# Loading the first four units' r and k without their gap rows, with three smaller moves beside it

## The chip, the cores and the metric

The kernel runs on one core of a Trainium2 chip. The metric is device time in microseconds (us) of one execution; less is better. The shown time of a kernel is the median of several executions.

## The reference, cut to what matters

Three stages follow one another. The first is a recurrence with a decaying state (4 batches, 8 heads, 768 steps, head size 48); the other two are feed-forward blocks over the 3072 tokens (384 to 2048 to 384).

```
for t in range(S):
    kt, vt, rt = (k[:, :, t], v[:, :, t], r[:, :, t])
    cur = np.einsum('bhd,bhe->bhde', u[None] * kt, vt)
    y[:, :, t] = np.einsum('bhd,bhde->bhe', rt, state + cur)
    state = w[None, :, :, None] * state + np.einsum('bhd,bhe->bhde', kt, vt)
h = x @ w_in;  g = h * np.tanh(softplus(h));  x = g @ w_out
h = np.maximum(x @ w_in, 0.0);  out = h * h @ w_out
```

## The kernel before

**Units.** The recurrence is done in chunks of 128 steps. A unit is one chunk of one batch: 6 chunks by 4 batches give 24 units; units 0 to 3 are the first chunk, and the feed-forward work can only begin when their y is there. For a unit, r and k lie transposed in a tile rk of 112 partitions by 1024 float32: even heads in rows 0 to 47, odd heads in rows 64 to 111, and rows 48 to 63, the gap rows, are zeros that come from memory with the rest. One transfer brings a tile (448 KB). The values v (192 KB) and the natural-order k (192 KB) of units 0 to 3 are further transfers; later units load a whole nat tile (576 KB).

**The work on a unit of the first chunk.** `products` (L474 VectorE, L479 TensorE, L482 VectorE) multiplies r by k over all 112 rows and sums them with u to the diagonal dg. `rk_scale` (L462, VectorE) scales the 112 rows with powers of the decay, the table E, which `tables` (L284 to L304, VectorE) makes from w. `scores` (L541, TensorE) multiplies k by r from rows 0 to 47 and 64 to 111. `fill` writes dg on the anti-diagonal of a tile A, for even heads (e = 0) and odd heads (e = 1): by ScalarE in four instructions (L514) or by VectorE in one (L520). `select` (L550, VectorE) puts the scores into A by a mask. `y_pe` (L598, L601, TensorE) makes y, and `y_out` (L685, L687, L694) splits it in two parts, xh and xl, which feed the first block.

**The feed-forward blocks.** The hidden dimension has 16 tiles of 128; a column of 512 tokens against a tile j is a step i. A step's up product is nine matrix products (`mm3`, L815 to L817: high by high, high by low, low by high, for three depths). After the gate function (ScalarE L852, L862, L871; VectorE L877) the result g is split in ghi (L909) and glo (L914), and the down product is again nine matrix products. For the steps in `FULL` it isn't: g stays float32, is not split, and the down product is three float32 products (L939), which the profile records as six. Before, `FULL` holds steps 0 to 6. Weights come as 64-bit floats (raw, 768 KB a tile) and are turned into high and low parts by ScalarE (L371, L377, L412) and VectorE (L381, L388, L410, L415).

**What sets the order.** `Plan.order` (L144) simulates the engines with a duration and a due time for each item, and the program is issued in the order that comes out. Every engine then runs its queue in that order; an instruction that waits holds up all behind it. All of the loads concerned are issued by SyncE (SP), through `dma` (L261). A semaphore wait comes from each true dependence. Units 0 to 3 load by `load_unit` (L436), with due times -180 + 10 n; raw weights of the first block follow with -140 + j; each natural k has -136.5 + n. `first` (L309) issues the table of w before all that. VectorE first zeroes `idle` (L329), on which TensorE runs 11 products (L327) while the loads come. GpSimd (POOL) zeroes four small pieces of the states (L318) and the tile pads (L655), and copies parts of v into pads (L663).

Of the kernel before, what the change touches and what calls it, by code (L numbers as in the profile page):

```python
# [20 lines left out]
B, H, S, D = 4, 8, 768, 48  # L21
# [16 lines left out]
GROUP_OF = [(sum(GROUPS[:g]), n) for g, n in enumerate(GROUPS) for _ in range(n)]  # L38
HIGH, WHIGH = 32, 2
WACT = frozenset(range(5, 9))  # L40
FULL = frozenset(range(0, 7))


class Tl:
# [165 lines left out]
def rwkv_moe_kernel(ctx: ExitStack, tc: tile.TileContext, good, rk, nat, wuT, wrow, ub, cst, w1, w2, out):  # L210
    nc = tc.nc
# [46 lines left out]
    add = plan.add  # L258

    def dma(o, i, eng=nc.sync):  # L260
        eng.dma_start(out=o, in_=i)  # L261
# [59 lines left out]
    idle = const.tile([128, 512], BF16, name="idle")  # L321
    T_idle = fixed(idle, "idle")
# [3 lines left out]
        for _ in range(n):  # L326
            nc.tensor.matmul(o, idle[:, 0:128], idle, start=True, stop=True, skip_group_check=True)  # L327

    add("DVE", 0.2, -199, lambda: nc.vector.memset(idle, 0.0), w=[T_idle])  # L329
    t = R["acc2"].new([128, 512], F32, "idle_ps")  # L330
    add("PE", 4.5, -199, lambda t=t: busy(t.get(), 11), r=[T_idle], w=[t])

# [8 lines left out]
    t = R["at"].new([128, NP, 128], F32, "tps")  # L341
# [14 lines left out]
    def convert(layer, j, due, load_due):  # L356

        raw = R[f"w{j}"].new([128, 768, 2], U32, f"raw{layer}_{j}")
        t, hi, lo = parts(layer, j)
        f = WF[layer, j] = R["wf"].new([128, 768], F32, f"wf{layer}_{j}")  # L360
        src = (w1, w2)[layer - 1][j]
# [31 lines left out]
            )  # L393

        it = add("SP", 0.786, load_due, load, w=[raw])
        if layer == 2:
            gates.append((it, int(load_due)))
        elif j >= 6:
            gates.append((it, -1))
# [28 lines left out]


    ups = {}  # L430
    units = [(c, b) for c in range(NCH) for b in range(B)]
    NU = len(units)
    U = {}
# [2 lines left out]
    def load_unit(n, due):  # L436
        u = U[n] = {}
        if n < B:
            t = u["rk"] = R[("rk", "rk", "w12", "w14")[n]].new((HP, 2, NP, C), F32, f"rk{n}")
            v = u["nat"] = R[("nat", "w11", "w13", "w15")[n]].new((128, 3, H, D), F32, f"nat{n}")  # L440
            u["k"], u["v"] = (v.part(lambda ap, i=i: ap[:, i]) for i in (1, 2))
            src = rk[n, :, 0:2 * NP * C].rearrange("q (i p t) -> q i p t", i=2, p=NP)
            add("SP", 0.69, due, lambda: dma(t.get(), src), w=[t])
            add("SP", 0.29, due, lambda: dma(u["v"].get(), nat[n][:, 2]), w=[u["v"]])
            ups[-1] = add("SP", 0.29, -136.5 + n, lambda: dma(u["k"].get(), nat[n][:, 1]), w=[u["k"]])
            return
        for x, shape, src, mb in (("rk", (HP, 2, NP, C), rk[n, :, 0:2 * NP * C].rearrange("q (i p t) -> q i p t", i=2, p=NP), 0.69), ("nat", (128, 3, H, D), nat[n], 0.88)):
            t = u[x] = R[x].new(shape, F32, f"{x}{n}")
            def load(t=t, src=src):
                dma(t.get(), src)  # L450

            it = add("SP", mb, due, load, w=[t])
            gates.append((it, int(due)))
        u["k"] = u["v"] = u["nat"]
# [50 lines left out]
    def fill(n, e, due):  # L505

        u = U[n]
        A = u["A", e] = R["glo" if n in (1, 3) else "A"].new([128, NP, C], F32, f"A{n}_{e}")

        def f():  # L510
            a = A.get()
            for p in range(NP):
                h = 2 * p + e
                nc.scalar.activation(a[:, p, :], anti, AF.Copy, scale=u["dg"][:, h:h + 1])  # L514

        if 2 <= n < B and e or units[n][0] == 1 and not e:

            def g():
                d = u["dg"].ap.rearrange("q (p e) -> q e p", e=2)[:, e, :]
                nc.vector.tensor_tensor(  # L520
                    A.get(), anti[:, None, :].to_broadcast([128, NP, C]), d[:, :, None].to_broadcast([128, NP, C]), ALU.mult
                )

            add("DVE", 0.69, due, g, r=[u["dg"], T_cst], w=[A])
            return
        add("ACT", 1.56, due, f, r=[u["dg"], T_cst], w=[A])
# [509 lines left out]
    t = R["acc2"].new([128, 512], F32, "idle_ps2")  # L1036
# [307 lines left out]
```

## Time and profile before

| what | value |
|---|---|
| median of three executions | 915.09 us (912.25 to 916.12) |
| the profiled execution, its own time | 915.5 us |
| its span in the profile | 913.7 us |
| TensorE busy | 901.0 us of it, 99% |
| VectorE busy / ScalarE busy | 549.2 us / 582.6 us |
| read from memory / written to it | 100.27 MB / 29.88 MB |

The span runs from the first instruction to the last; the profiled execution's own time has 1.8 us around it. A busy share is an average over the whole span: the first 30 us are another stage than the rest, and each stage has to be read by itself. In the profile's lists, an idle time in square brackets stands before the instruction that it delayed, with what released that instruction. SPq is the queue of SyncE, which issues transfers.

### The profile page before, as it was taken

What the parts mean: (1) busy time and instruction counts of PE and PEld (TensorE: products, weight loads), DVE (VectorE), ACT (ScalarE), POOL (GpSimd) and SP (SyncE); (2) the same over time, 40 slices, a digit from 0 to 9 for tenths busy, and PEclk for the clock granted to TensorE, in tenths of its full rate; (3) what the DMA queues carried; (4) which work ended last, traced back from release to release, by engine and by line L of the source; (5) the groups of instructions that cost most, each with busy time, mean ns of one, the idle gap of its engine ahead of it and who ended that gap; (6) DMA issues with size and microseconds to landing.
All of it is one profiled execution on the core that took longest, in us unless ns stands there. A gap on an engine that the chain in (4) does not pass through costs nothing.

```text
span 913.7 us, 13422 instructions
## 1 busy us (share of the span) xinstructions
PE 901.0 (99%) x5228; PEld 756.4 (83%) x5228; DVE 549.2 (60%) x911; ACT 582.6 (64%) x1059; POOL 3.9 (0%) x13
## 2 busy tenths in 40 slices
PE   8999999999999999999999999999999999999997
PEld 6666788789898988788888888888888888899997
DVE  8999947999343448678885323224677876211212
ACT  5999768896455567778775554544677866544442
POOL 1000000000000000000000000000000000000000
PEclk9999999999999999999999999999999999999999
DMA  9996416994226654022665110655300355200001
GB/s 288 350 374 239 155 63 221 368 393 193 69 83 221 224 186 149 1 56 75 214 219 185 47 56 17 203 199 193 104 9 1 103 185 195 70 1 1 35 0 39
DMA packets 34537, 132.09 MB, mean 145 GB/s; under 512 B 3905, under 2 KB 8258, under 8 KB 34466
## 3 DMA queue, kind: packets, MB, share of 16 engines
q1 hardware_dynamic: 34178, 130.76, 42.0%
q8 instruction: 43, 0.70, 0.3%
q10 hardware_dynamic: 288, 0.39, 0.1%
q14 instruction: 28, 0.23, 0.1%
HBM read 100.27 MB, written 29.88 MB: 142 GB/s over the span
## 4 chain that ended last, share of the span: by engine, by line
PE 91%; DMA 5%; DVE 2%; ACT 1%; issue 0%; SPq 0%; DVEq 0%
PE h L815 14%; PE h L817 14%; PE h L816 14%; PE acc L976 7%; PE acc L978 7%; PE acc L977 7%; PE acc L815 7%; PE acc L817 6%; PE acc L816 6%; DMA nat<-in_nat_dram 3%; PE sc L541 2%; PE y L611 2%; PE acc L939 1%; PE y L588 1%; DMA raw<-in_w_dram 1%; PE y L644 1%
## 5 line engine op out<-in xcount | busy, mean ns | idle before, releaser
L914 DVE TENSOR_TENSOR glo<-g,ghi 128x512 fp32r<-128x512 f32 x96 | 66.4, 692 | 216.9 <-ACT ghi L906 213.4
L922 ACT ACTIVATE e<-h 128x512 f32<-128x512 f32 x96 | 57.4, 597 | 174.5 <-PE h L817 174.5
L906 ACT ACTIVATE ghi<-e 128x512 fp32r<-128x512 f32 x96 | 59.7, 622 | 19.9 <-PE acc L977 19.9
L914 DVE TENSOR_TENSOR glo<-e,ghi 128x512 fp32r<-128x512 f32 x89 | 60.2, 691 | 17.0 <-ACT ghi L911 14.5
L923 ACT ACTIVATE g<-e 128x512 f32<-128x512 f32 x96 | 60.7, 632 | 2.9
L897 DVE TENSOR_TENSOR e<-e,r 128x512 f32<-128x512 f32 x64 | 44.2, 691 | 26.2 <-ACT r L896 25.9
L892 ACT ACTIVATE e<-h 128x512 f32<-128x512 f32 x64 | 37.9, 592 | 32.3 <-PE h L817 32.0
L514 ACT ACTIVATE A<-cst_sb,dg 128x128 f32<-128x128 f32 x168 | 52.9, 392 | 2.7 <-DVE dg L482 2.6
L911 ACT ACTIVATE ghi<-e 128x512 fp32r<-128x512 f32 x64 | 40.2, 628 | 21.7 <-DVE e L890 21.6
L895 ACT ACTIVATE r<-e 128x512 f32<-128x512 f32 x64 | 40.1, 627 | 15.9 <-DVE e L884 15.9
L887 DVE SCALAR_TENSOR_TENSOR r<-e,r 128x512 f32<-128x512 f32 x64 | 44.2, 691 | 1.7
L890 DVE SCALAR_TENSOR_TENSOR e<-r,h 128x512 f32<-128x512 f32 x64 | 43.9, 686 | 1.7
L976 PE MATMUL acc<-w,ghi 128*128 128x384 f32 x128 | 44.2, 345 | 0.0
L978 PE MATMUL acc<-w,glo 128*128 128x384 f32 x128 | 43.2, 337 | 0.0
L977 PE MATMUL acc<-w,ghi 128*128 128x384 f32 x128 | 43.1, 337 | 0.0
L893 ACT ACTIVATE e<-e 128x512 f32<-128x512 f32 x64 | 40.4, 631 | 1.7
L896 ACT ACTIVATE r<-r 128x512 f32<-128x512 f32 x64 | 40.3, 629 | 1.4
L550 DVE COPY_PREDICATED A<-cst_sb,sc 128x512 f32<-128x512 int32 x48 | 33.9, 734 | 12.1 <-PE sc L541 12.1
L815 PE MATMUL h<-xh_a,w 128*128 128x512 f32 x96 | 39.7, 413 | 0.0
L462 DVE TENSOR_TENSOR rk<-rk,E 112x1024 f32<-112x1024 f32 x24 | 29.3, 1221 | 17.2 <-DMA rk<-in_rk_dram 17.2
L815 PE MATMUL h<-xh_b,w 128*128 128x512 f32 x96 | 37.7, 393 | 0.6 <-DVE e L877 0.6
L816 PE MATMUL h<-xl_a,w 128*128 128x512 f32 x96 | 37.5, 391 | 0.2 <-DVE xl_a L694 0.2
(510 smaller groups left out, 2495.6 us busy)
## 6 DMA issues: line engine op xcount, KB each, us to landing
raw<-in_w_dram SPq DMA_DIRECT2D x32, 768.0 KB, 10.4
wd<-w SPq DMA_DIRECT2D x32, 768.0 KB, 9.0
nat<-in_nat_dram SPq DMA_DIRECT2D x20, 576.0 KB, 5.1
rk<-in_rk_dram SPq DMA_DIRECT2D x24, 448.0 KB, 5.0
out_dram<-o SPq DMA_DIRECT2D x22, 192.0 KB, 2.0
w_0r<-wd SPq DMA_DIRECT2D x4, 768.0 KB, 4.3
w_1r<-wd SPq DMA_DIRECT2D x4, 768.0 KB, 5.7
w_2r<-wd SPq DMA_DIRECT2D x4, 768.0 KB, 5.5
```

The costliest lines, as they stand in the source:

```text
L514: nc.scalar.activation(a[:, p, :], anti, AF.Copy, scale=u["dg"][:, h:h + 1])
L815: nc.tensor.matmul(o, wh, xh, start=first, stop=False, skip_group_check=True)
L816: nc.tensor.matmul(o, wh, xl, start=False, stop=False, skip_group_check=True)
L817: nc.tensor.matmul(o, wl, xh, start=False, stop=last, skip_group_check=True)
L887: nc.vector.scalar_tensor_tensor(r.ap, e.ap, 2.0, r.ap, ALU.subtract, ALU.mult)
L906: add("ACT", 0.63, due, lambda: nc.scalar.activation(hi.get(), square.ap, AF.Square), r=[square], w=[hi])
L914: lambda: nc.vector.tensor_tensor(lo.get(), g.ap, f32v(hi.ap), ALU.subtract), r=[g, hi], w=[lo],
L922: add("ACT", 0.59, d, lambda: nc.scalar.activation(e.get(), h.ap, AF.Relu), r=[h], w=[e])
L923: add("ACT", 0.63, d + 0.2, lambda: nc.scalar.activation(g.get(), e.ap, AF.Square), r=[e], w=[g])
L976: nc.tensor.matmul(o, hi[:, sl], h_, start=(j == 0), stop=False, skip_group_check=True)
L977: nc.tensor.matmul(o, hi[:, sl], l_, start=False, stop=False, skip_group_check=True)
L978: nc.tensor.matmul(o, lo[:, sl], h_, start=False, stop=(j == NF - 1), skip_group_check=True)
```

## The change

- Units 0 to 3 load rk in two transfers, rows 0 to 47 and rows 64 to 111 (192 KB each). Rows 32 to 63 are zeroed on the chip before: by VectorE for units 0 and 1, by GpSimd for units 2 and 3. The loads wait for that, since rows 32 to 47 are written by both. The zeroing of `idle` gets an earlier due time, so that it stays first on VectorE.
- The order of these loads is fixed: rk0, rk1, v0, rk2, v1, rk3, v2, v3, then the first raw weights. Before, it was rk0, v0, rk1, v1, rk2, v2, rk3, v3. The first raw weights come ahead of the natural k of all four units, the other raw weights of the first block after v3.
- `FULL` loses step 6: six steps stay unsplit.
- The fill of unit 1's odd heads goes from ScalarE to VectorE.

```diff
-FULL = frozenset(range(0, 7))
+FULL = frozenset(range(0, 6))
...
-    add("DVE", 0.2, -199, lambda: nc.vector.memset(idle, 0.0), w=[T_idle])
+    add("DVE", 0.2, -240, lambda: nc.vector.memset(idle, 0.0), w=[T_idle])
...
         it = add("SP", 0.786, load_due, load, w=[raw])
+        if layer == 1 and not j:
+            order = [first_loads[k] for k in sorted(first_loads)] + [it]
+            for p, q in zip(order, order[1:]):
+                q["after"].append(p)
+            for q in later:
+                q["after"].append(it)
+        elif layer == 1:
+            it["after"].append(first_loads[B + 0.5])
...
-            add("SP", 0.69, due, lambda: dma(t.get(), src), w=[t])
-            add("SP", 0.29, due, lambda: dma(u["v"].get(), nat[n][:, 2]), w=[u["v"]])
+
+            def load():
+                for q in (0, 64):
+                    dma(t.get()[q:q + D], src[q:q + D])
+
+            if n >= 2:
+                add("POOL", 0.95, -230 + n, lambda: nc.gpsimd.memset(t.get()[32:64], 0.0), w=[t])
+            else:
+                add("DVE", 0.4, -230 + n, lambda: nc.vector.memset(t.get()[32:64], 0.0), w=[t])
+            first_loads[n] = add("SP", 0.59, -180 + 2 * n, load, w=[t])
+            first_loads[n + 1.5] = add("SP", 0.29, -177 + 2 * n, lambda: dma(u["v"].get(), nat[n][:, 2]), w=[u["v"]])
             ups[-1] = add("SP", 0.29, -136.5 + n, lambda: dma(u["k"].get(), nat[n][:, 1]), w=[u["k"]])
+            later.append(ups[-1])
...
-        if 2 <= n < B and e or units[n][0] == 1 and not e:
+        if 1 <= n < B and e or units[n][0] == 1 and not e:
```

## Rows read from the trace of the kernel before

**Rows 1.** The page, busy time of each engine in the span.
```profile
PE 901.0 (99%) x5228; PEld 756.4 (83%) x5228; DVE 549.2 (60%) x911; ACT 582.6 (64%) x1059; POOL 3.9 (0%) x13
```

**Rows 2.** Waits of TensorE, whole span: waited for, us in total, times, longest.
```profile
PE y L598 <- DVE A L550: 2.7, 1, 2.7
PE acc L939 <- DVE g L877: 1.9, 2, 1.0
```

**Rows 3.** The chain that ended last, first 60 us: start, us, what.
```profile
29.55 14.25 DMA nat<-in_nat_dram
...
51.68 0.61 DVE g L877
...
52.33 2.84 PE acc L939 x6
```

**Rows 4.** Windows of 5 us: PE, PEld, DVE, ACT, POOL busy, PEclk, DMA share, GB/s.
```profile
5.00:10.00 5.00, 5.00 (x37) 3.95 (x35) 3.28 (x8) 0.49 (x1) 1.64 (x2) 1.00 1.05 266
...
15.00:20.00 5.00, 4.85 (x72) 4.28 (x70) 4.93 (x9) 4.00 (x11) 0.00 (x0) 1.00 1.04 402
...
25.00:30.00 5.00, 5.00 (x45) 3.98 (x42) 4.61 (x7) 3.66 (x7) 0.00 (x0) 0.74 1.05 396
```

**Rows 5.** VectorE in order of time, first 45 us: start, us, what [idle before, releaser].
```profile
0.88 0.27 DVE L329 MEMSET idle<- 128x256 uint32 x1 [0.88 <-PEq L1327]
2.37 0.17 DVE L284 TENSOR_SCALAR wu_sb<-wu_sb 112x4 f32<-112x4 f32 x1 [1.22 <-DMA wu_sb<-in_wuT_dram]
...
5.44 0.16 DVE L304 COPY w<-Ex 112x4 f32<-112x4 f32 x1
6.74 0.69 DVE L474 TENSOR_TENSOR pr<-rk 112x512 f32<-112x512 f32 x1 [1.13 <-DMA rk<-in_rk_dram]
...
9.24 0.69 DVE L474 TENSOR_TENSOR pr<-rk 112x512 f32<-112x512 f32 x1 [0.55 <-DMA rk<-in_rk_dram]
...
11.73 0.69 DVE L474 TENSOR_TENSOR pr<-rk 112x512 f32<-112x512 f32 x1 [0.54 <-DMA rk<-in_rk_dram]
...
18.01 0.69 DVE L520 TENSOR_TENSOR A<-cst_sb,dg 128x512 f32<-128x512 f32 x1
...
43.89 0.56 DVE L493 TENSOR_TENSOR nat<-nat,ub_sb 128x384 f32<-128x384 f32 x1 [1.45 <-DMA nat<-in_nat_dram]
```

**Rows 6.** SyncE's queue in order of time: start, us, transfers issued.
```profile
1.67 0.43 SPq L261 DMA_DIRECT2D rk<-in_rk_dram  x1
2.15 0.43 SPq L261 DMA_DIRECT2D nat<-in_nat_dram  x1
...
6.73 3.62 SPq L261 DMA_DIRECT2D raw<-in_w_dram  x4
```

**Rows 7.** GpSimd and ScalarE in order of time.
```profile
7.59 1.38 POOL L655 MEMSET pads<- 128x1536 f32 x1 [6.60 <-PE tps L336]
...
13.15 2.45 ACT L514 ACTIVATE A<-cst_sb,dg 128x128 f32<-128x128 f32 x8 [0.65 <-DVE dg L482]
```

**Rows 8.** TensorE in order of time: down products of steps 6 and 8.
```profile
80.16 2.73 PE L939 MATMUL acc<-g,wf 128*128 128x512 f32 x6
82.82 0.44 PE L588 MATMUL y<-rk,S 48*64 48x128 f32 x8
...
91.19 0.40 PE L815 MATMUL acc<-ghi,w 128*128 128x512 f32 x1
91.43 0.40 PE L816 MATMUL acc<-glo,w 128*128 128x512 f32 x1
...
93.36 0.38 PE L541 MATMUL sc<-rk 48*128 48x128 f32 x2
```

**Rows 9.** VectorE in order of time, splits of steps 8 and 9.
```profile
89.43 0.44 DVE L909 CAST ghi<-e 128x512 fp32r<-128x512 f32 x1
...
90.22 1.30 DVE L914 TENSOR_TENSOR glo<-e,ghi 128x512 fp32r<-128x512 f32 x2
```

**Rows 10.** One window, 45 to 113 us, columns as in rows 4.
```profile
45.00:113.00 68.00, 66.88 (x452) 47.34 (x453) 67.95 (x112) 58.25 (x94) 0.00 (x0) 1.00 0.67 252
```

More of the change, by code (lines that the diff above doesn't have):

```diff
@@ L430, in rwkv_moe_kernel @@
     ups = {}
+    first_loads, later = {}, []
     units = [(c, b) for c in range(NCH) for b in range(B)]
```

## The prediction

> **What bounds the kernel now.** I read the page's busy times first: TensorE is busy 901.0 of 913.7 us [rows 1], so only what moves its work as a whole, shortens it, or removes one of its waits can count. Its waits come next [rows 2]: 2.7 us once for the select of the first chunk, and 1.9 us in two waits for g. That is nearly all there is to win besides an earlier start.
>
> The chain of waits says what sets the first 52 us [rows 3]. It runs through transfers, the last of which is the nat tile of unit 4, issued at 29.55 and 14.25 us on its way. VectorE sits idle 1.45 us for it until 43.89 [rows 5], and the gate products (g, L877) queued behind it reach TensorE late; at 52.33 TensorE goes on [rows 3]. From there to the end it is busy nearly without a gap. So the arrival of nat4 plus VectorE's work behind it sets the end; anything earlier counts only if it moves that arrival, or eats more than VectorE's 1.45 us.
>
> The windows show why transfers matter: the DMA share is full (1.05) both from 5 to 10 us, at 266 GB/s, and from 15 to 20 us, at 402 GB/s [rows 4]. The slow stretch is that of rk and v. VectorE waits for rk0 until 6.74, for rk1 until 9.24, for rk2 until 11.73 [rows 5]: a step of 2.5 us for rk and v together, 640 KB or 0.655 MB, 262 GB/s. By bytes (448 of 640) rk's part of it is 1.75 us.
>
> **The change part by part.**
>
> *Zeroing on the chip.* A zeroing of 256 elements a row took VectorE 0.27 us [rows 5]; 1024 elements are worked out as 1.08 us. VectorE is then free of the first at 0.88 + 0.27 + 1.08 = 2.23 and of the second at 3.31. SyncE issued rk0 at 1.67 [rows 6]; now it waits there for the first zeroing, until about 2.3, and everything behind it in its queue waits too: **+0.6 us** on the start of all loads. The ends are 0 (the zeroing takes under 0.5 us) and 1.6 (both zeroings come ahead of it, 3.31 less 1.67). The engines had nothing but the small constants to move by then, so nothing hides it. rk1 would be issued at 2.3 and two more issues of 0.48 (the spacing in [rows 6]), 3.26, against 3.31: hidden by rk0's own transfer. The decay tables start at 3.31 instead of 2.37 and so end near 6.5 instead of 5.6 [rows 5]; they are needed after the first product, at 6.74 + 0.69. Hidden, with 0.9 us of cover; past that it would cost one for one. GpSimd's two take 1024/1536 of 1.38 us each [rows 7], 0.92, and end before 3; rk2 is the sixth issue, after 4.6. Hidden. TensorE's first tables wait likewise; nothing needs them early.
>
> *Twice four loads instead of four.* Four more issues of 0.48 us are 1.9 us of SyncE's time. At that spacing the eight loads are issued by 5.5; then it stood until rk0 had landed (6.74 [rows 5]) before the first raw weights, at 6.73 [rows 6]. With the two small tables before them done, eight seem to stand open at a time. Eight halves of 192 KB are 6 us of work at 262 GB/s: the engines don't run dry, so the issues cost nothing. Were they to run dry, it would be the 1.9.
>
> *Fewer bytes.* 64 KB a unit, 256 KB or 0.26 MB in all. If the rate stays 262 GB/s a pair of halves takes 384/448 of 1.75, 1.50 us: 0.25 a unit, 1.0 us in all. But the same full engines move 402 GB/s of weights, so it isn't bytes alone that fill them during rk. A load of 48 rows, all within one half of the partitions, is shown by no row. The nearest rows for the dear end: a half-range load at half of the weights' rate, 201 GB/s, makes 0.393 MB / 201 = 1.96 us a pair, +0.21 a unit, **+0.84** in all; at the extreme a half takes as long as a whole does now, +7.0. Between 1.50 and 1.96 I take the middle, 1.73, which is the 1.75 of now: **0**.
>
> The Trainium skill, page "SBUF — State Buffer", in the section "Can I just issue two DMAs to hit both halves?", speaks against this edit: one load from partition 0 on and one from 64 on were only 6% faster together than one, since each reaches half of the ports. With its 196 GB/s for 64 partitions that is an estimate of 208 GB/s, 1.89 us a pair, +0.6 instead of my 0. No row here loads one half alone, so the trace neither bears it out nor refutes it.
>
> *Values one load later.* v0 comes behind rk1, about 1.7 us later; it is read only after the fill and the selects of its unit. rk1 to rk3 come ahead of one v each (0.75 us). VectorE waited 0.55 and 0.54 us for rk1 and rk2 [rows 5]; those go, and VectorE's next wait takes them up.
>
> *One more fill on VectorE.* +0.69 us there [rows 5], ScalarE loses four of the eight in 2.45 us [rows 7], 1.2 us. VectorE is busy 4.93 of 5 us around it [rows 4], so the first chunk's select comes later and TensorE's 2.7 us wait grows; TensorE then runs partly at the lower of its two clocks, as before (granted 0.74 between 25 and 30 us [rows 4]). All this is upstream of nat4: 0.6 and 0.69 are 1.29, under the 1.45 us of idle before 43.89. **0**; without that cover 0.69.
>
> *Step 6 split.* TensorE: the float32 down product takes from 80.16 to 82.82, 2.66 us; a split one from 91.19 to 93.36, 2.17 [rows 8]: −0.49. VectorE: a cast of 0.44 and half of 1.30 [rows 9], +1.09, in a stretch in which it is busy 67.95 of 68 us [rows 10]. Step 8's glo is done at about 90.87 [rows 9] and read at 91.43 [rows 8]: 0.56 us of slack, against 1.09 + 0.49 that the two engines move apart. At worst TensorE waits 1.02, a net +0.53; at best −0.49. VectorE's weight work may be reordered around it: I take the middle, **0**.
>
> **Sum.** +0.6 for the wait of the first load, carried by the chain of transfers to nat4 and on to TensorE. The profiled execution took 915.5 us (1.8 around its span of 913.7), 0.4 over the median. 915.09 + 0.6 = **915.7 us**; its own ends, 0 to 1.6 for the wait and 0.5 either way for step 6, give 914.6 to 917.2. A measurement of this kernel can hardly tell less than 0.5%, 4.6 us, from no change.
>
> **Rivals.**
>
> *Bytes decide* (faster). The rate stays and the pair costs 1.50 us: −1.0 + 0.6, and step 6 gives its 0.49 because VectorE's order leaves the glo in time: −0.9, **914.2 us**. For it: the DMA engines are full without a gap, so less to move is less time. Against: the wait at the start takes back more than half. At the far end nat4 comes so early that both waits for g vanish, −1.9 − 0.49, 912.7.
>
> *Half a range at a time* (slower). Each half load reaches only part of the ways into the memory, and the engines queue for it: +0.84 to the chain and +0.6 at the start, **916.5 us**; the place is SyncE's first six loads, and it decides as soon as a pair takes over 1.75 us. For it: loads of rk already run 1.5 times slower than weights at the same DMA share. Against: no row shows a half load. By the skill's section named above the sum would be 916.3. Twice this price, with step 6 and the fill uncovered, is 918.6.
>
> *VectorE becomes the bound* (slower). It gets 0.69 early and 1.09 in its full stretch; if nat4 is no longer the last to arrive, both come out at TensorE: 0.6 + 0.69 + 0.53, **916.9 us**. For it: rows 10. Against: the 1.45 us of idle.
>
> **How the numbers follow.** The forecast (no net gain) 0.42, bytes 0.33, half ranges 0.17, VectorE 0.08. The range goes from the far end of the second to that of the third, 912.7 to 918.6. Beyond 0.5% on the fast side would need three times the waits for g gone, or the stretch of low clock with them: 0.04. On the slow side half loads far dearer than half the weights' rate: 0.08. Between, 0.88.
>
> **What would show it.** In the changed profile: VectorE's zeroings of 32 by 1024 near 1.08 us; rk0's first issue near 2.3 instead of 1.67; the first product (L474) at about 7.3 instead of 6.74; the third at most 1.7 us behind the second, against 2.49; the first raw weights landing within 1 us of 16.6; nat4's reader (L493) at about 44.5; TensorE's waits for g again near 2 us; six rather than seven of the float32 down products. I am wrong if the zeroings take half of that, if the products come before 6.5, or if L493 moves by over 1 us either way.

## The result, and the profile after

The changed kernel took **921.12 us** (median of 22 runs, 914.70 to 923.54) beside 916.12 (22 runs, 912.25 to 920.03) for the kernel before, run beside it. The ratio is 1.0059, with a 95% interval of 1.0045 to 1.0072: slower by 5.4 us, where 0.6 was forecast, and beyond the range. The profiled execution took 921.36 us, with a span of 919.6, against 915.5 and 913.7 before. Line numbers of the old code move by 19 from L462 on (L474 is now L493, L493 is L512, L815 is L834, L939 is L958).

The page of the changed kernel: busy times, and the granted TensorE clock in 40 slices.

```profile
PE 904.8 (98%) x5229; PEld 761.0 (83%) x5231; DVE 552.5 (60%) x916; ACT 580.7 (63%) x1055; POOL 6.6 (1%) x15
...
PEclk7899999999999999999999999999999999999999
```

TensorE is busy 3.8 us longer than in [rows 1], with one product more on record: of the 5.9 us that the span grew, 3.8 are added busy time (slower products, less what the split of step 6 saves) and 2.1 are idle time. The clock is below 9 in the first two slices; before, all 40 are 9. Windows of 5 us, first of the changed kernel (columns as in [rows 4]):

```profile
5.00:10.00 5.00, 3.15 (x25) 2.64 (x23) 3.83 (x10) 0.49 (x1) 2.04 (x2) 1.00 1.02 223
10.00:15.00 5.00, 4.67 (x37) 3.52 (x39) 4.97 (x9) 3.38 (x12) 1.72 (x4) 0.62 1.05 283
15.00:20.00 5.00, 5.00 (x32) 3.72 (x28) 3.38 (x5) 2.85 (x4) 0.54 (x1) 0.50 1.04 399
20.00:25.00 5.00, 5.00 (x36) 4.76 (x38) 3.21 (x7) 2.09 (x5) 0.00 (x0) 0.50 1.04 396
25.00:30.00 5.00, 4.50 (x52) 4.28 (x51) 3.71 (x8) 2.78 (x8) 0.00 (x0) 0.68 1.04 393
```

The same view of the kernel before, with windows that were not shown ahead of the prediction:

```profile
5.00:10.00 5.00, 5.00 (x37) 3.95 (x35) 3.28 (x8) 0.49 (x1) 1.64 (x2) 1.00 1.05 266
10.00:15.00 5.00, 4.79 (x50) 3.70 (x50) 4.46 (x8) 4.30 (x15) 1.84 (x3) 1.00 1.05 288
...
20.00:25.00 5.00, 2.27 (x29) 1.96 (x29) 5.00 (x9) 5.00 (x10) 0.00 (x0) 0.92 1.03 391
```

The clock column is the one to read, with one warning. The clock record in the trace begins only when the clock first rises, at 7.1 us before and at 4.3 after. Until then a window shows 1.00, although the products on zeros (listed below) take 0.44 us each before, about twice as long as later. From that rise on TensorE held the full 2.4 GHz until 24.2 us before. After, the clock falls at 11.2 us and stays at 0.50, the 1.2 GHz level, until 28.2. Twice (1 − PEclk) times the length of each window, added up, gives the time at the lower level behind the first rise: 3.4 us in the first 30 before, 17.0 after. With the time up to the first rise, it is about 10.5 us before and 21.4 after. Being busy did not bring the clock back here: from 15 to 25 us TensorE is busy all the time in the changed kernel and stays at 0.50. And one window ahead of the fall TensorE, which before had been busy for all of its 5 us, is busy for 3.15.

What it waited for there stands in TensorE's own order of time (start, us, what, idle before and releaser), changed kernel:

```profile
1.20 4.07 PE L327 MATMUL idle_ps<-idle 128*128 128x512 bf16 x11 [1.20 <-DVE idle L329]
6.30 1.15 PE L336 MATMUL tps<-cst_sb,Ex 112*128 112x112 f32 x8 [1.02 <-DVE Ex L293]
...
9.32 1.02 PE L498 MATMUL dgp<-wu_sb,pr 112*128 112x2 f32 x8 [0.77 <-DVE pr L493]
...
35.81 0.50 PE L835 MATMUL h<-xl_a,w 128*128 128x512 f32 x1 [1.16 <-DVE xl_a L713]
...
57.16 5.42 PE L958 MATMUL acc<-g,wf 128*128 128x512 f32 x12
...
72.72 0.50 PE L834 MATMUL h<-xh_a,w 128*128 128x512 f32 x1 [1.79 <-DVE g L896]
...
74.89 2.74 PE L958 MATMUL acc<-g,wf 128*128 128x512 f32 x6
```

The same view of the kernel before:

```profile
1.20 4.88 PE L327 MATMUL idle_ps<-idle 128*128 128x512 bf16 x11 [1.20 <-DVE idle L329]
5.87 1.65 PE L336 MATMUL tps<-cst_sb,Ex 112*128 112x112 f32 x8
...
30.80 0.50 PE L816 MATMUL h<-xl_a,w 128*128 128x512 f32 x1 [0.22 <-DVE xl_a L694]
...
69.61 2.74 PE L939 MATMUL acc<-g,wf 128*128 128x512 f32 x6
```

Before, the eleven products on zeros (L327) ran until 6.08 us, past the moment at which VectorE had finished what TensorE needs of the decay tables (L293, at 5.19), and TensorE went on without a gap. After, it stands 1.02 us for the tables at 5.3 us, and 0.77 for unit 1's product at 8.5. Then come the long products. The up projection's first product with xl_a, which waits for VectorE, starts at 35.81 instead of 30.80: 5.0 us late. The third float32 down product starts at 57.16 instead of 52.33 [rows 3], 4.8 late, the fifth at 74.89 instead of 69.61, 5.3 late. So nearly the whole loss exists by 36 us; what follows carries it to the end.

Where the two waits come from is VectorE's order of time, changed kernel, to be read against [rows 5]:

```profile
1.41 0.91 DVE L460 MEMSET rk<- 32x1024 f32 x1 [0.27 <-issue]
2.48 0.91 DVE L460 MEMSET rk<- 32x1024 f32 x1 [0.16 <-issue]
3.43 0.17 DVE L284 TENSOR_SCALAR wu_sb<-wu_sb 112x4 f32<-112x4 f32 x1
...
6.50 0.16 DVE L304 COPY w<-Ex 112x4 f32<-112x4 f32 x1
6.75 0.69 DVE L493 TENSOR_TENSOR pr<-rk 112x512 f32<-112x512 f32 x1
8.48 0.69 DVE L493 TENSOR_TENSOR pr<-rk 112x512 f32<-112x512 f32 x1 [1.04 <-DMA rk<-in_rk_dram]
9.10 2.42 DVE L481 TENSOR_TENSOR rk<-rk,E 112x1024 f32<-112x1024 f32 x2
...
47.37 0.56 DVE L512 TENSOR_TENSOR nat<-nat,ub_sb 128x384 f32<-128x384 f32 x1
```

and two lines of the kernel before that [rows 5] leaves out:

```profile
4.31 0.88 DVE L293 TENSOR_TENSOR Ex<-Ex 112x256 f32<-112x256 f32 x2
...
7.46 1.22 DVE L462 TENSOR_TENSOR rk<-rk,E 112x1024 f32<-112x1024 f32 x1
```

Two zeroings of 0.91 us push the tables from 2.37 to 3.43, and the start of their last step from 5.44 to 6.50. The second product waits for its transfer, but the data are not late: it comes at 8.48, where it came at 9.24 before. What comes late is the scaling of unit 0. Before, it stood between the two products, at 7.46; now the planner has put it behind the second, at 9.10. So TensorE has no scores of unit 0 to make while it waits for unit 1's product: they start at 10.73 instead of 8.92. Nat4's reader, which had 1.45 us to spare, comes at 47.37 instead of 43.89 and waits for no transfer any more: VectorE is late because TensorE is, and nat4 no longer sets anything.

The transfers themselves kept their time. SyncE's queue, changed kernel, against [rows 6]:

```profile
2.35 1.85 SPq L261 DMA_DIRECT2D rk<-in_rk_dram  x4
...
9.23 2.95 SPq L261 DMA_DIRECT2D raw<-in_w_dram  x4
```

The first rk is issued at 2.35 instead of 1.67, as forecast. ScalarE's first read of raw weights (L371), which waits for their transfer, starts at 16.46; before it was 16.59.

TensorE's waits over the whole span, changed kernel, against [rows 2]. Beside the four that stand in its order of time above (1.79, 1.16, 1.02 and 0.77 us), two more are of note:

```profile
PE h L834 <- DVE e L896: 0.9, 1, 0.9
...
PE y L617 <- DVE A L569: 0.5, 1, 0.5
```

The select's wait of 2.7 us shrank to 0.5, and TensorE goes on from it at 29.33 instead of 23.49. The six add up to 6.2 us, against 4.6 for the two of [rows 2] and 1.2 in four smaller waits of the kernel before.

**The clock differs from execution to execution.** Over the 115 executions of the kernel before that were made beside the experiments, time and mean granted clock go together: 46 at 0.997 or more took 913.1 us in the mean, 14 at 0.991 or less 918.8, and the fitted line costs 0.7 us for each 0.001. The changed kernel's mean clock is 0.9893, against 0.9946. By that line the 0.0053 are an estimated 3.7 us of the 5.4. (This mean, too, leaves out the time up to the first rise.) Two of its 22 executions held 0.997, and took 914.7 and 916.0.

### The profile page after: what moved, and what is told of

Read it like the earlier page. It is cut to its first block, busy times and chain, and to the rows that moved or that the text cites. A ratio compares the mean times of both kernels' runs of the same rounds, so it can differ in the third digit from the quotient of the medians.

```text
span 919.6 us, 13435 instructions
## 1 busy us (share of the span) xinstructions
PE 904.8 (98%) x5229; PEld 761.0 (83%) x5231; DVE 552.5 (60%) x916; ACT 580.7 (63%) x1055; POOL 6.6 (1%) x15
## 4 chain that ended last, share of the span: by engine, by line
PE 89%; DVE 7%; DMA 1%; ACT 1%; issue 1%; SPq 0%; DVEq 0%
PE h L834 14%; PE h L836 13%; PE h L835 13%; PE acc L995 7%; PE acc L997 7%; PE acc L996 7%; PE acc L834 6%; PE acc L836 6%; PE acc L835 6%; PE sc L560 3%; PE y L630 2%; PE y L607 1%; DVE wf L388 1%; DVE w L423 1%; DVE wf L381 1%
## 5 line engine op out<-in xcount | busy, mean ns | idle before, releaser
L834 PE MATMUL h<-xh_a,w 128*128 128x512 f32 x96 | 39.9, 415 | 2.1 <-DVE g L896 1.8
L834 PE MATMUL h<-xh_b,w 128*128 128x512 f32 x96 | 37.7, 393 | 0.9 <-DVE e L896 0.9
L481 DVE TENSOR_TENSOR rk<-rk,E 112x1024 f32<-112x1024 f32 x24 | 29.4, 1229 | 14.4 <-DMA rk<-in_rk_dram 14.4
```

The lines of the kernel that those rows point to most:

```text
L834: nc.tensor.matmul(o, wh, xh, start=first, stop=False, skip_group_check=True)
```

## The experiments

Ratios are to the kernel before, run beside it. "Clock" is the mean granted clock of the executions, with that of the kernel before beside them in brackets. "Rise" is when the clock record of the profiled execution begins, "low" the time at the lower clock level behind that in its first 36 us, worked out as above; "gap" is 5 us less TensorE's busy time from 5 to 10 us there.

| kernel | median us (range, runs) | before (runs) | ratio, 95% | clock | profiled us | rise us | low us | gap us |
|---|---|---|---|---|---|---|---|---|
| before | | | | 0.9946 | 915.5 | 7.1 | 3.4 | 0.0 |
| after | 921.12 (914.70–923.54, 22) | 916.12 (22) | 1.0059, 1.0045–1.0072 | 0.9893 | 921.36 | 4.3 | 17.0 | 1.85 |
| e1_warm | 918.39 (915.29–921.98, 12) | 915.38 (35) | 1.0030, 1.0009–1.0050 | 0.9935 (0.9943) | 920.38 | 5.4 | 13.6 | 1.27 |
| e2_warm_twice | 917.00 (915.97–921.49, 12) | 915.38 (35) | 1.0026, 1.0004–1.0048 | 0.9954 (0.9943) | 917.28 | 7.0 | 6.8 | 0.0 |
| e3_late_tables | 914.09 (911.95–919.72, 12) | 915.38 (35) | 0.9994, 0.9972–1.0016 | 0.9955 (0.9943) | 913.06 | 5.6 | 3.5 | 0.21 |
| e4_pool_zero | 917.80 (916.17–922.80, 12) | 915.38 (35) | 1.0035, 1.0011–1.0060 | 0.9919 (0.9943) | 916.17 | 6.9 | 6.8 | 0.27 |
| e5_whole | 915.27 (914.87–917.73, 12) | 913.94 (22) | 1.0011, 0.9994–1.0028 | 0.9952 (0.9948) | 915.18 | 4.8 | 6.8 | 0.22 |
| e6_seven | 920.32 (916.98–922.14, 9) | 913.94 (22) | 1.0064, 1.0039–1.0089 | 0.9894 (0.9948) | 916.98 | 6.6 | 3.4 | 0.76 |
| e7_fill_act | 924.13 (920.74–925.00, 6) | 913.94 (22) | 1.0095, 1.0065–1.0124 | 0.9885 (0.9948) | 923.23 | 4.5 | 17.2 | 2.31 |
| e8_loads_only | 921.25 (917.54–922.60, 9) | 913.94 (22) | 1.0057, 1.0033–1.0081 | 0.9902 (0.9948) | 922.60 | 6.2 | 20.5 | 1.27 |
| e9_split_rows | 919.08 (915.94–924.18, 12) | 914.38 (35) | 1.0043, 1.0019–1.0066 | 0.9917 (0.9947) | 916.94 | 5.7 | 6.7 | 0.28 |
| e10_split_cols | 917.44 (914.38–922.63, 12) | 914.38 (35) | 1.0027, 1.0004–1.0050 | 0.9935 (0.9947) | 918.15 | 6.0 | 6.8 | 0.49 |
| e11_filled | 913.60 (912.83–917.23, 12) | 914.38 (35) | 0.9997, 0.9978–1.0016 | 0.9966 (0.9947) | 913.47 | 4.7 | 3.4 | 0.15 |
| e12_fill_only | 917.55 (915.85–919.47, 12) | 914.38 (35) | 1.0028, 1.0011–1.0045 | 0.9933 (0.9947) | 917.47 | 6.0 | 6.8 | 0.41 |
| e13_short_warm | 920.37 (918.84–922.13, 12) | 915.52 (23) | 1.0063, 1.0044–1.0082 | 0.9988 (0.9945) | 920.29 | 27.3 | 3.4 | 0.23 |
| e14_true_costs | 922.81 (917.90–926.85, 12) | 915.52 (23) | 1.0081, 1.0057–1.0104 | 0.9891 (0.9945) | 918.75 | 4.7 | 6.7 | 1.13 |

### Is it TensorE's idle time at the start?

**e1_warm**: the changed kernel with five more products on zeros ahead of the tables.

```diff
-    add("PE", 4.5, -199, lambda t=t: busy(t.get(), 11), r=[T_idle], w=[t])
+    add("PE", 4.5, -199, lambda t=t: busy(t.get(), 16), r=[T_idle], w=[t])
```

> Changed kernel with 16 instead of 11 of the products on zeros ahead of the decay tables, which fills TensorE's idle 1.02 us at 5.3 us and nothing else. Theory (clock): that idle time is what lets the granted clock fall at 11.4 us; with it filled, the mean granted clock is 0.995 or more, the first chunk's y is done by 29 us instead of 32, and the time is 914 to 916.5 us. If the second idle time (0.77 us at 8.5 us) is enough by itself, the clock still falls, 0.987 to 0.990, and the time stays at 920 to 922. Rival (order): VectorE's new order, with unit 1's product waiting ahead of unit 0's scaling, and the slower half loads cost the time; the products change nothing, 920 to 922 us whatever the clock does. Rival (step 6): the split of step 6 costs it behind 75 us; 920 to 922 us and the stretch up to 60 us as before.

**e2_warm_twice**: e1, and four more products on zeros while unit 1's product is awaited (the step of L498, which so depends on the zeroed tile too).

```diff
             o = ps.get()
+            if n == 1:
+                busy(o, 4)
             for p in range(NP):
```

> As the run with 16 products, and four more products on zeros ahead of unit 1's diagonal products, where TensorE stands idle 0.77 us at 8.5 us. Theory (clock): both idle times gone, mean granted clock 0.995 or more in nearly every execution, 913.5 to 916 us. Rival (order) and rival (step 6): 920 to 922 us.

Measured: 1.0030 and 1.0026 instead of 1.0059, so about half of the loss comes back. That is less than either theory had, and both intervals still touch that of the change. The mean clock comes back further, from 0.9893 to 0.9935 and 0.9954. TensorE's order of time in e1:

```profile
1.20 5.67 PE L327 MATMUL idle_ps<-idle 128*128 128x512 bf16 x16 [1.20 <-DVE idle L329]
6.71 1.04 PE L336 MATMUL tps<-cst_sb,Ex 112*128 112x112 f32 x8
...
10.02 1.02 PE L498 MATMUL dgp<-wu_sb,pr 112*128 112x2 f32 x8 [1.29 <-DVE pr L493]
```

The gap before the tables is gone, the second grew to 1.29 us, and the lower level still takes 13.6 us. In e2 no gap is left, and it takes 6.8. Not one product of the kernel's own work was taken away or moved to another engine: only idle time was filled. What stays, 0.26% (0.04 to 0.48), comes at no lower mean clock than that of the kernel before, and in the profiled execution without idle time of TensorE from 5 to 10 us. The filler's own time may be part of it: the tables' products start at 7.51 us in e2's profile, at 6.30 in the changed kernel's.

**e3_late_tables**: the kernel before, with VectorE kept busy ahead of the tables by two writes that nothing reads.

```diff
     def tables():
+        for _ in range(2):
+            nc.vector.memset(Ex[0:32], 0.0)
```

> Kernel before, with two zeroings of 32 by 1024 on VectorE ahead of the decay tables (into the tables' own space, overwritten after): the tables come about 1 us later, and loads, order, fills and step 6 are as before. Theory (clock): TensorE stands idle about 1 us at 5.9 us, ahead of the tables' products; if that alone decides, the granted clock falls near 11 us and the time is 918 to 922 us; if it takes both idle times of the changed kernel, the clock stays and the time is 915 to 917. Rival (order) and rival (step 6): nothing of theirs is in it, so 915 to 916.5 us.

Measured: no difference (0.9994, 0.9972 to 1.0016). What TensorE needs of the tables was there at 6.07 us, 0.88 later than before and 0.18 earlier than in the changed kernel (6.25). In the profiled execution the products on zeros lasted until 5.9 us, so TensorE waited only 0.21 us; with products that take 4.07 us, as in the changed kernel's profile, the wait would be an estimated 0.85. How long it was in the other eleven is not known. So tables that come nearly as late as in the changed kernel cost nothing measurable by themselves, and the full microsecond of idle time was not shown to arise.

**e13_short_warm** makes idle time in the other way: the kernel before with five products on zeros instead of eleven. Loads, tables and all of VectorE's work stay.

```diff
-    add("PE", 4.5, -199, lambda t=t: busy(t.get(), 11), r=[T_idle], w=[t])
+    add("PE", 4.5, -199, lambda t=t: busy(t.get(), 5), r=[T_idle], w=[t])
```

> Kernel before with 5 instead of 11 products on zeros at the start: TensorE stands idle some 2.5 us ahead of the tables' products, and nothing else differs. Theory (clock): the idle time alone is enough, the mean granted clock falls from 0.9946 to 0.991 or less and the time rises to 917 to 922 us, with the loads and VectorE's order of the kernel before. Rival (the low clock of the changed kernel is a side effect of late data): the loads and VectorE come as before, so 914 to 916 us.

Measured: 1.0063 (1.0044 to 1.0082), as much as the whole change costs. TensorE's order of time in it:

```profile
1.20 2.31 PE L327 MATMUL idle_ps<-idle 128*128 128x512 bf16 x5 [1.20 <-DVE idle L329]
5.23 2.05 PE L336 MATMUL tps<-cst_sb,Ex 112*128 112x112 f32 x8 [1.72 <-DVE Ex L293]
7.07 1.73 PE L479 MATMUL dgp<-wu_sb,pr 112*128 112x2 f32 x8
...
38.38 0.50 PE L816 MATMUL h<-xl_a,w 128*128 128x512 f32 x1 [0.73 <-DVE xl_a L694]
...
58.36 2.84 PE L939 MATMUL acc<-g,wf 128*128 128x512 f32 x6 [0.62 <-DVE g L877]
```

An idle time of 1.72 us at the start (most of it before 5 us, so not in the table's gap), and the first group of diagonal products takes 1.73 us where it takes 1.05 in the kernel before. The product that waits for xl_a comes at 38.38 instead of 30.80, and the third down product at 58.36 instead of 52.33 [rows 3]. So a start with less work for TensorE, alone, with loads as they were, can cost what the change cost. Its course is another, though. The changed kernel's clock rose at 4.3 us and fell at 11.2; here it did not rise until 27.3, and with the time up to the rise TensorE spent 30.7 of the first 36 us at the lower level, against 21.4 in the changed kernel and 10.5 before. That is twice the extra time for the same loss, so this run does not show that the change's whole loss is of this kind. The mean clock of 0.9988 is not the 0.991 or less of the theory, since the record leaves out the time up to the rise.

**The pair that the executions give by themselves.** e6 (below) differs from the changed kernel in step 6 alone; TensorE's first 557 products are the same in both. In its profiled execution the clock took another way. TensorE's order of time, e6:

```profile
1.21 4.87 PE L327 MATMUL idle_ps<-idle 128*128 128x512 bf16 x11 [1.21 <-DVE idle L329]
6.30 1.29 PE L336 MATMUL tps<-cst_sb,Ex 112*128 112x112 f32 x8 [0.22 <-DVE Ex L293]
...
8.94 1.02 PE L498 MATMUL dgp<-wu_sb,pr 112*128 112x2 f32 x8 [0.54 <-DVE pr L493]
...
30.25 0.51 PE L835 MATMUL h<-xl_a,w 128*128 128x512 f32 x1 [0.89 <-DVE xl_a L713]
...
52.02 5.42 PE L958 MATMUL acc<-g,wf 128*128 128x512 f32 x12
...
67.19 0.50 PE L834 MATMUL h<-xh_a,w 128*128 128x512 f32 x1 [1.79 <-DVE g L896]
...
81.55 2.74 PE L958 MATMUL acc<-g,wf 128*128 128x512 f32 x6
```

The same eleven products on zeros took 4.87 us here and 4.07 in the changed kernel's profile, so the first gap was 0.22 us instead of 1.02; the second was 0.54 instead of 0.77. The lower level lasted 3.4 us instead of 17.0, the wait for xl_a ended at 30.25 instead of 35.81, and the execution took 916.98 instead of 921.36. The same program start, 4.4 us apart, with another course of the clock. Its 52.02 is even ahead of the 52.33 of before; the 1.5 us by which it is slower than the profile of before arise after that, in the stretch with the 1.79 us wait for g: its seventh float32 down product starts at 81.55, against 80.16 [rows 8].

Which of the two gaps went with the long stretch can be read from e8 (below), whose first 96 products are those of e6 too. TensorE's order of time in it:

```profile
1.20 4.88 PE L327 MATMUL idle_ps<-idle 128*128 128x512 bf16 x11 [1.20 <-DVE idle L329]
6.30 1.15 PE L336 MATMUL tps<-cst_sb,Ex 112*128 112x112 f32 x8 [0.22 <-DVE Ex L293]
...
9.53 1.74 PE L498 MATMUL dgp<-wu_sb,pr 112*128 112x2 f32 x8 [1.05 <-DVE pr L493]
```

The first gap is e6's 0.22 us, but the second is 1.05, and the lower level lasted 20.5 us. In the profiles of e1 and e7 as well a second gap of over 1 us (1.29 and 1.23) goes with a long stretch, whether the first is filled (e1) or not (e7, 0.93). Leaving e13 aside, the profiles with a long stretch are those with 0.77 to 1.29 us of idle time at this place; the others have 0 to 0.54 there. These are single executions, so it is a pattern and no proof.

### Which part of the change makes the idle time, and what else does it cost?

**e4_pool_zero**: the changed kernel with all four zeroings on GpSimd, so that the tables start as early as before.

```diff
-            if n >= 2:
-                add("POOL", 0.95, -230 + n, lambda: nc.gpsimd.memset(t.get()[32:64], 0.0), w=[t])
-            else:
-                add("DVE", 0.4, -230 + n, lambda: nc.vector.memset(t.get()[32:64], 0.0), w=[t])
+            add("POOL", 0.95, -230 + n, lambda: nc.gpsimd.memset(t.get()[32:64], 0.0), w=[t])
```

> Changed kernel with all four zeroings on GpSimd (0.91 us each, one after the other): VectorE's tables start at 2.4 us again, the first load of rk is issued near 1.8 instead of 2.35. Theory (clock): no idle time ahead of the tables, mean granted clock 0.994 or more, 913.5 to 916 us. Rival (order) and rival (step 6): the half loads and the step are as in the changed kernel, 919 to 922 us.

**e5_whole**: the changed kernel with whole loads of rk, gap rows and all, and no zeroing. The new order of the loads, the fill and step 6 stay.

```diff
-                for q in (0, 64):
-                    dma(t.get()[q:q + D], src[q:q + D])
...
+                dma(t.get(), src)
...
-            first_loads[n] = add("SP", 0.59, -180 + 2 * n, load, w=[t])
+            first_loads[n] = add("SP", 0.69, -180 + 2 * n, load, w=[t])
```

> Changed kernel with rk of units 0 to 3 loaded whole again (no zeroing, 448 KB in one transfer), the new order of the loads, step 6 split and the fill kept. Over the executions so far, the changed kernel is 2.0 us above the kernel before at the same mean granted clock (916.9 against 914.9 at 0.995), and its mean clock is 0.989 against 0.994. Theory (clock, from the zeroings' delay and the new order of the first chunk): without zeroing and with the planner's other order the clock is 0.993 or more and the time 914 to 917.5 us. Theory (half loads are slow): the same, and the products of units 1 to 3 come no later than in the changed kernel though more is loaded. Rival (step 6 or the fill costs it): 919 to 922 us still.

**e6_seven**: step 6 whole again. **e7_fill_act**: the fill of unit 1 back on ScalarE. **e8_loads_only**: both, which leaves the loads and the zeroing.

```diff
-FULL = frozenset(range(0, 6))
+FULL = frozenset(range(0, 7))
...
-        if 1 <= n < B and e or units[n][0] == 1 and not e:
+        if 2 <= n < B and e or units[n][0] == 1 and not e:
```

> Changed kernel with step 6 unsplit again (seven float32 tiles). Theory (first chunk): the clock stays at 0.987 to 0.991, since nothing before 70 us differs; TensorE's wait of 1.8 us for g at 72 us is then either gone, and the time is 1 to 2 us less (919 to 920.5), or still there, and the time is 921 or a little more. Rival (step 6 decides): 915 to 917 us.

> Changed kernel with the fill of unit 1's odd heads back on ScalarE. Theory (first chunk's order and its zeroings): idle times ahead of the tables and of unit 1's diagonal remain, clock 0.987 to 0.992, 919 to 922 us. Rival (the fill on VectorE holds up the selects and so lets the clock fall): clock 0.994 or more and 915 to 917 us.

> Changed kernel with seven float32 tiles and the fill on ScalarE: only the half loads, their zeroing and their order are left of the change. Theory (the loads' part decides): clock 0.987 to 0.992 and 918 to 922 us. Rival (step 6 and the fill decide): as the kernel before, 914 to 916.5 us at 0.993 to 0.996.

Measured: the loads with their zeroing alone (e8, 1.0057) cost what the whole change costs; without them (e5, 1.0011) no loss is measurable. With the zeroings off VectorE (e4, 1.0035) the gap falls to 0.27 us and 0.24% come back, 2.2 us, though the intervals overlap and the theory had 913.5 to 916 us; its first product waits 0.72 us for rk at 7.10, since its load is held back all the same. Nor did e4 put the tables back. They start at 2.37 as before, but two of their steps (L288, L289) took 0.88 and 0.81 us instead of 0.17, while GpSimd was still zeroing (0.75 to 4.41 us), and they end at 6.38, against 5.60 before and 6.66 in the changed kernel. For step 6 no difference is measured (1.0064 against 1.0059); with the fill on ScalarE it stands between e7 and e8, 1.0095 and 1.0057, whose intervals overlap. The fill on VectorE does not cost here: putting it back makes 1.0095 and 924.13 us, more than the theory's 922, though that interval (1.0065 to 1.0124) touches the one of the change.

### Do half loads cost time of their own?

**e9_split_rows**: e5 with each rk in two transfers, rows 0 to 63 and 64 to 111. **e10_split_cols**: e5 with each rk in two transfers of all 112 rows, r and then k. Both carry the same bytes as the whole load, without zeroing.

```diff
-                dma(t.get(), src)
+                for q in (slice(0, 64), slice(64, HP)):
+                    dma(t.get()[q], src[q])
```

```diff
-                dma(t.get(), src)
+                for i in range(2):
+                    dma(t.get()[:, i], src[:, i])
```

> Changed kernel without zeroing: rk of units 0 to 3 with all 112 rows, 448 KB, in two transfers by rows, 0 to 63 and 64 to 111. Beside the run with whole loads (915.3 us; 313, 281 and 379 GB/s in the windows 5:8, 8:11, 11:14; products at 5.86, 7.73, 9.59) only the split differs. Theory (half ranges are slow): the rate from 5 to 11 us falls to 210 to 250 GB/s, VectorE's first product comes at 7 us or later, the mean clock falls under 0.993, and the time is 917 to 922 us. Rival (the zeroing alone costs it): the rate stays near 300, products by 6.2, 915 to 916.5 us.

> As the run split by rows, but split by columns: each of the two transfers has all 112 rows and half of each row (r, then k; 224 KB). Theory (half ranges are slow): as many transfers, but the whole range each, so the rate from 5 to 11 us stays at 270 or more, the first product comes before 6.6 us and the time is 914.5 to 917 us. Rival (two transfers in place of one cost it, or SyncE's four more issues): as split by rows, 917 to 922 us.

Windows of 3 us, columns as in [rows 4], first of e9:

```profile
5.00:8.00 3.00, 2.72 (x19) 2.23 (x18) 2.29 (x5) 0.49 (x1) 1.12 (x1) 1.00 1.01 188
8.00:11.00 3.00, 2.92 (x29) 2.09 (x29) 2.25 (x4) 1.65 (x6) 1.56 (x2) 1.00 1.07 225
```

and of e10:

```profile
5.00:8.00 3.00, 2.51 (x16) 1.95 (x14) 1.84 (x5) 0.49 (x1) 0.96 (x1) 1.00 0.99 276
8.00:11.00 3.00, 3.00 (x31) 2.46 (x32) 2.68 (x5) 1.62 (x6) 1.77 (x2) 1.00 1.08 266
```

The same bytes in as many transfers move at 206 GB/s (the mean of the two windows) when split by rows and at 271 when split by columns, with the DMA engines full in both. From 5 to 11 us every profiled execution with loads split by rows (after, e1, e2, e4, e6 to e9, e14) lies between 194 and 245 GB/s, and those with whole loads (before, e3, e5, e11 to e13) between 254 and 306. So, in these profiles, a load that lies in one half of the partitions is slower, and it is the rows, not the number of transfers. The Trainium skill, page "SBUF — State Buffer", section "Can I just issue two DMAs to hit both halves?", whose rule came to an estimate of 208 GB/s for this case, agrees with e9's 206 in size, though the 206 is of rk and v together. In time the two kernels are not told apart: 919.08 against 917.44, and the intervals of their ratios overlap. But e9, with no zeroing and no wait for the tables, is 0.43% slower than the kernel before (0.19 to 0.66) at a mean clock of 0.9917, and e5, with whole loads, is not (0.11%, −0.06 to 0.28); these two intervals overlap a little. In the profiles the third product waits for rk until 11.37 us in e9 and starts at 9.59 in e5. So half loads are a rival for a good part of the loss, and not excluded.

### What is left, and can it be had back?

**e12_fill_only**: the kernel before with the fill of unit 1 on VectorE, and nothing else.

```diff
-        if 2 <= n < B and e or units[n][0] == 1 and not e:
+        if 1 <= n < B and e or units[n][0] == 1 and not e:
```

> Kernel before with only the fill of unit 1's odd heads moved to VectorE. Theory: 0.69 us more on VectorE ahead of the first chunk's selects, covered by its idle 1.45 us at 43.9 us, so 914 to 916.5 us; moving it back in the changed kernel cost 3 us. Rival (the fill on ScalarE holds up the first chunk in the kernel before too): 912 to 914 us.

Measured: 1.0028, 2.6 us, which neither the theory nor the rival had. TensorE's order of time in it:

```profile
17.42 1.84 PE L479 MATMUL dgp<-wu_sb,pr 112*128 112x2 f32 x8 [2.02 <-DVE pr L474]
```

It isn't the 0.69 us of the fill. With other costs the planner writes another order, VectorE makes unit 3's product only at 16.60, and TensorE waits 2.02 us for it; the diagonal products behind that wait take 1.84 us instead of the 1.02 of before.

**e14_true_costs**: the changed kernel, with the planner told what the zeroings and the loads take.

```diff
-                add("DVE", 0.4, -230 + n, lambda: nc.vector.memset(t.get()[32:64], 0.0), w=[t])
+                add("DVE", 0.95, -230 + n, lambda: nc.vector.memset(t.get()[32:64], 0.0), w=[t])
...
-            first_loads[n] = add("SP", 0.59, -180 + 2 * n, load, w=[t])
+            first_loads[n] = add("SP", 0.69, -180 + 2 * n, load, w=[t])
```

> Changed kernel with the planner told what was measured: 0.95 instead of 0.4 for a zeroing on VectorE, 0.69 instead of 0.59 for a pair of half loads. VectorE then scales unit 0 ahead of unit 1's product, as in the kernel before. Theory (order): the 2 us that the changed kernel is longer at equal clock, and part of the low clock, come from an order made for loads that are faster than they are; 915 to 918.5 us, 0.992 or more. Rival (the late data alone: zeroing and half ranges): 919.5 to 922 us, 0.987 to 0.991.

Measured: 1.0081, no better, and slower than theory and rival had. The order of VectorE's first steps becomes that of before (product, scaling, product), and the waits come in other places. TensorE's order of time in it:

```profile
6.31 1.15 PE L336 MATMUL tps<-cst_sb,Ex 112*128 112x112 f32 x8 [0.87 <-DVE Ex L293]
...
16.93 1.02 PE L498 MATMUL dgp<-wu_sb,pr 112*128 112x2 f32 x8 [1.56 <-DVE pr L493]
```

So the planner's wrong costs for zeroings and loads are not the cause. This profile also bounds the idle theory: 0.87 us of it at 5.4, none ahead of unit 1's product, and the lower level came late and lasted only 6.7 us. That execution was a short one of its kernel, 918.75 us against a median of 922.81, and over all twelve the mean clock was 0.9891, as low as the changed kernel's. So either this execution escaped the long stretch, or the low clock of the others has another cause; they were not profiled.

**e11_filled**: the kernel before, with eight products on zeros ahead of the first chunk's values, where TensorE waits 2.7 us for the select [rows 2].

```diff
         def f():
+            if n == 2:
+                busy(ps[0].get(), 8)
```

> Kernel before, with eight products on zeros put ahead of unit 2's y, where TensorE waits 2.7 us for VectorE's selects at 20.8 us, ahead of the stretch of low clock from 24.2 to 27.6 us. Theory (clock): less low clock there, mean granted clock up from 0.9945 to 0.996 or more, and by 0.7 us per 0.001 of mean clock (the slope over the executions of the kernel before) 1 to 2 us less, 913 to 914.5 us. Rival (the clock is a side effect and the chain of transfers to the nat tile at 43.9 us sets the end): 914.5 to 916 us with the clock up or not.

Measured: 0.9997 (0.9978 to 1.0016), no difference in time, though the mean clock is the theory's: 0.9966, against 0.9947. In the profiled execution the lower level lay from 15.0 to 18.4 us, ahead of the place that was filled, with 3.4 us as before, so that profile says nothing of the filler. No version here is measurably faster than the kernel before.

## Why the prediction was wrong

**The step that failed** is that TensorE's start was put at nothing. Of the tables the prediction says "Hidden, with 0.9 us of cover" and "TensorE's first tables wait likewise; nothing needs them early"; of VectorE's waits for rk1 and rk2 it says that they go. The first was right for VectorE (the tables end at 6.66, the first product follows at 6.75). For TensorE no row stood behind it, and the rows were there: before, its products on zeros ended at 6.08, and what it needs of the tables was there at 5.19. Delayed by 1.06 us, to 6.25, the tables leave TensorE idle for 0.22 us where the products on zeros take 4.87 (e6's profile), and for 1.02 where they take 4.07, as in the changed kernel's. The second wait did not go either: the planner moved unit 0's scaling behind unit 1's product, and TensorE stood idle for another 0.77 us. These lengths are not the price. The price is the lower clock that followed: 17.0 us instead of 3.4 in the profile, at which products take up to twice as long. Filling the gaps brought the mean clock back to that of the kernel before and gave back about half of the time (e1, e2). So this step carries about half of the loss. The runs do not separate its two gaps: filling the first alone gave back nearly as much time as filling both, but late tables alone cost nothing measurable (e3), and in the profiles the long stretch goes with the second.

**"TensorE then runs partly at the lower of its two clocks, as before"** is the second failure, of the same kind: the 0.74 of [rows 4] was taken as a fixed feature, though filling TensorE's idle time changed the clock (e1, e2), and so did a shorter filler (e13). With it the argument of the cover fell. All losses were to lie upstream of nat4, behind VectorE's 1.45 us. The loss of 5.0 us at 35.81 is larger than that cover, and L512 came at 47.37 without waiting, where 44.5 was forecast and a miss of over 1 us was named as the sign of an error.

Step by step otherwise:
- *Zeroing*: 0.91 us each instead of 1.08, and the first begins at 1.41, not at 1.15, so the first issue at 2.35 meets the forecast 2.3 by two errors that cancel; but the +0.6 that this wait was to carry through the transfers to nat4 and on to the end did not arrive as such: the raw weights were read at 16.46, before at 16.59.
- *Twice four loads*: 1.85 us for four issues, and the DMA share stays full, 1.02 and 1.05. Right, nothing.
- *Fewer bytes*: 1.73 us a pair was taken, the middle of two bounds. From 5 to 11 us the changed kernel moved 226 GB/s, rk and v together, so a pair of 0.393 MB takes 1.74. Right in size, but by luck: no row stood behind the middle, and by e9's 206 it would be 1.91, near the dear end.
- *Values one load later*: VectorE's wait for rk2 went, as forecast; the one for rk1 grew from 0.55 us to 1.04, since no scaling stands ahead of it any more.
- *Third product at most 1.7 us behind the second*: it came 3.1 behind, at 11.58 after 8.48. But it waited for no transfer; VectorE did two scalings (L481) first. That sign was badly chosen, since order alone can break it.
- *Fill*: 0 was forecast. In the kernel before it costs 2.6 us (e12), by the planner's new order and not by its 0.69; in the changed kernel taking it out gains nothing (e7). A price that depends on the order around it can't be had from the duration of one instruction.
- *Step 6*: 0 forecast, no difference measured (e6).

Of the rivals, *half a range at a time* had its mechanism right, shown by e9 against e10, and a price of 0.84 us that was small beside the clock's, unless it is also what keeps e4 and e9, with half loads and no wait for the tables, 0.35 and 0.43% slower. *Bytes decide* was wrong: the rate did not stay at 262. *VectorE becomes the bound* was right in one place: the waits of 1.16 us for xl_a and 1.79 for g are VectorE's. e6, where the clock was nearly that of before, keeps 1.5 us of loss in the stretch with the second one. No rival had TensorE's idle time at the start in it, so the chance of over 0.5% slower, 0.08, was too low, and the range ended 2.5 us short of the median.

**What stays open**: the other half. With the idle time at the start filled (e2), 0.26% are left. The half loads (e9, 0.43% without zeroing), the fill (e12, 0.28%), the order that the planner writes around both and the filler's own time can each give that much, the intervals overlap, and e14 shows that the planner's costs for loads and zeroings are not the key. Nor was a version tried with the zeroings on GpSimd and the gaps filled at once.

## What to carry to other kernels

Filler products ahead of TensorE's first real work are part of its schedule: whoever delays that work must see when the filler ends, and lengthen it. Here an idle microsecond of TensorE at the start went with a loss that the clock column of the later windows shows and its length does not, and an engine "busy 98%" hid that loss, since slow products count as busy. When a planner orders the work, cost an edit by the order that it writes, not by the duration of the added instruction.

## What the runs showed of the hardware

- One program spreads by its clock: the kernel before took 911.6 to 921.1 us, and 0.7 us more for each 0.001 less of mean granted clock. Eleven equal products on zeros took 4.07 us in one execution and 4.87 in another, since TensorE's speed rose sooner in the first.
- The recorded clock does not cover the start: e13 shows a mean of 0.998 and 1.00 in every window up to 30 us, while its products took nearly twice their usual time until 27.3. There only their durations tell the level.
- Whole loads of the same 112 rows, DMA engines full, moved between 254 and 306 GB/s from 5 to 11 us in six profiled executions.
